# A shorter prologue and three short superblocks at the head of a banded-convolution, gate and two-projection kernel

## The chip, the cores and the metric

The kernel runs on one core of one Trainium2 chip. The metric is the device time of one execution in microseconds (us). Beside it each kernel has one profiled execution, whose trace gives the span from the first to the last instruction and the granted TensorE clock. PE is TensorE (PEld its weight loads), DVE VectorE, ACT ScalarE, POOL GpSimd, and SP the engine that here only issues DMAs. "Record" means one row of the trace.

## The reference

x is (8, 4224, 192) in float32. First a causal convolution of 7 taps with one kernel per head (8 heads of 24 channels, softmax over the taps), then a gated projection:

```python
# _attn_ref: w = softmax(weight, axis=-1); K = 7, H = 8
x_unf = x_pad[:, idx, :].reshape(B, S, K, H, group)
out = np.einsum('hk,bskhg->bshg', w, x_unf)
# _moe_ref on that output, K = 5
for k in range(K):
    gate_pre += conv_w[k][None, None, :] * xp[:, k:k + S, :]
gate = 1.0 / (1.0 + np.exp(-gate_pre))
val = x @ w_val
return (gate * val @ w_out).astype(np.float32)
```

x and the 7-tap weight are float32; conv_w, w_val and w_out are float64, and the kernel gets their bits as pairs of 32-bit words.

## The kernel before, in words

**Layout.** The eight sequences are laid end to end as two rows of 16926 tokens that run side by side. The 192 channels don't fit 128 partitions evenly: tile x1 holds 128 channels of both rows one behind the other, tile x2 the other 64 channels, row 0 on its lower 64 partitions and row 1 on its upper.

**Superblocks and steps.** The tokens are cut into superblocks g (list NJS; the number is windows of 122 tokens per fifth). A superblock of 5 has 1506 tokens in three steps of 502, of 3 has 896 in two steps of 448, of 2 has 606 in steps of 304 and 302. Before there are 13 superblocks and 35 steps.

**The convolution** (conv_unit) is a product with a band matrix: a window of 128 tokens by 120 columns (24 channels by 5 windows) is the stationary operand, the head's band (128x122) the moving one. Each such product is two records in the trace. Up to four windows form a unit in one bank of PSUM; ACT copies the unit to tile e, and when a head is complete, scatter sends it by DMA from e to x1 and x2: heads 0 to 4 in one transfer to x1, heads 5 to 7 in two or four smaller ones. A superblock of 5 has 40 such products (10 units), of 3 has 24 (6 units), of 2 has 16 (4 units). Heads go in the order QUADS: 6, 7, 5, 0, then 1, 2, 3, 4. The windows come from HBM by load_x into a ring of XBUFS buffers; load i waits until the products that read its buffer's former content are done.

**The main loop** runs over steps n. For step n PE makes the products v = x·w_val (three single-precision-rounded products for high and low parts, and a float32 part in columns), for step n-1 the products o with w_out; ACT opens and closes gates (gate_open scales by tap 0, gate_close is the sigmoid), DVE adds the other four taps (gate_taps) and multiplies (gated), POOL makes the low parts (split1, split2). Then come due[n] units of the convolution of the superblock LAG = 2 further on. gate_open(n+2, 0) stands in the middle of step n on ACT and waits for the scattered x1 of the superblock of step n+2. The order on each engine is that of the code, written out by hand.

**The prologue.** Band and weights are prepared: band is exp(taps - max), with -1e30 outside of the band, multiplied by 1/sum (rs). decode turns the float64 bits into a float32 value and a residual on DVE; put adds them into the weight tile; cast makes the rounded high part (ACT) and the low part (DVE). The convolution of superblocks 0 and 1 is interleaved with the decoding; then the loop begins.

```python
NJS = [2, 3] + [5] * 10 + [2]
PER_LOAD = {2: 2, 3: 1, 5: 1}
XBUFS, EBUFS = 6, 3
LAG = 2
BY_POOL = 3
```

Of the kernel before, what the change touches and what calls it, by code (L numbers as in the profile page):

```python
# [19 lines left out]
WIN = 122  # L20
# [8 lines left out]

NJS = [2, 3] + [5] * 10 + [2]


def half(n):
# [15 lines left out]
def room(n):  # L51
    return min(reach(n), NS * fifth(n)) - HALO
# [7 lines left out]
assert 0 < LEFT <= min(502, room(NJS[-1])) and LEFT % 2 == 0  # L60
NG = len(NJS)
PARTS = [BLOCKS[n] for n in NJS[:-1]] + [TAIL]
TOKS = [sum(p) for p in PARTS]
STEPS = []
# [16 lines left out]
PERM += [h * HC + i for i in range(HC) for h in (6, 7)]  # L81
PERM += [5 * HC + i for i in range(8, HC)]
QUADS = ((6, 7, 5, 0), (1, 2, 3, 4))
PER_LOAD = {2: 2, 3: 1, 5: 1}
XBUFS, EBUFS = 6, 3
LAG = 2
BY_POOL = 3


@with_exitstack  # L90
def kernel(
# [39 lines left out]
    def load_x(upto):  # L131
        while loaded[0] < min(upto, len(loads)):
            i = loaded[0]
            loaded[0] += 1
            g, hs, o = loads[i]
            f = len(hs) * NJS[g] * M
            t = xtiles[i] = xin.tile([WK, NMAX * M], F32, tag="x", name=f"x_{i}")
            nc.sync.dma_start(t[:, :f], xw[o : o + WK * f].rearrange("(p f) -> p f", f=f))

    w0 = cp.tile([128, NH, KW], F32, name="w0")
    nc.sync.dma_start(w0, hw)
    band = cp.tile([WK, NH, WIN], F32, name="band")
    for q in range(2):
        nc.sync.dma_start(band[:, 4 * q : 4 * q + 4, :], bw[:, 4 * q : 4 * q + 4, :])
# [15 lines left out]
    def load_raw(name):  # L162
        nc.sync.dma_start(raw[name][1], raw[name][2])

    load_raw("cw")
    load_raw("wv")
    load_x(4)
    load_raw("wo")
    load_x(XBUFS)

    one = cp.tile([128, 1], F32, name="one")
    nc.vector.memset(one, 1.0)
    warm = cp.tile([128, 1], F32, name="warm")
# [7 lines left out]
    nc.vector.tensor_reduce(out=mx, in_=w0, op=ALU.max, axis=mybir.AxisListType.X)  # L181
    w1 = cp.tile([128, NH, KW], F32, name="w1")
    nc.vector.tensor_tensor(out=w1, in0=w0, in1=wide(mx, KW), op=ALU.subtract)
    w2 = cp.tile([128, NH, KW], F32, name="w2")
    nc.scalar.activation(w2, w1, AF.Exp)
    halves = [slice(4 * q, 4 * q + 4) for q in range(2)]
    for q in halves:
        nc.vector.tensor_tensor(out=band[:, q], in0=band[:, q], in1=wide(mx, WIN, q), op=ALU.subtract)
        nc.scalar.activation(band[:, q], band[:, q], AF.Exp)
# [6 lines left out]
    for q in halves:  # L196
        nc.vector.tensor_tensor(out=band[:, q], in0=band[:, q], in1=wide(rs, WIN, q), op=ALU.mult)  # L197
    warm2 = cp.tile([128, 1], F32, name="warm2")
    nc.scalar.activation(warm2, rs[:, 0:1], AF.Sigmoid)

    tmp = [scratch(2 * D, 0 if i < 3 else 1) for i in range(4)]

    def decode(name, n):

        lo, hi = raw[name][0][:, :, 0], raw[name][0][:, :, 1]
        ex, ta, tb, res = (t[:, :n] for t in tmp)
        res = res.bitcast(F32)
        v = nc.vector
        SHR, SHL = ALU.logical_shift_right, ALU.logical_shift_left
        AND, OR, XOR = ALU.bitwise_and, ALU.bitwise_or, ALU.bitwise_xor  # L210

        v.tensor_scalar(out=ex, in0=hi, scalar1=20, scalar2=0x7FF, op0=SHR, op1=AND)
# [4 lines left out]
        v.scalar_tensor_tensor(out=ta, in0=ta, scalar=0x40000000, in1=tb, op0=XOR, op1=AND)
        v.tensor_tensor(out=ta, in0=ta, in1=ex, op=OR)
        v.scalar_tensor_tensor(out=ta, in0=hi, scalar=-0x80000000, in1=ta, op0=AND, op1=OR)

        v.tensor_scalar(out=tb, in0=ta, scalar1=-0x800000, scalar2=None, op0=AND)
        v.scalar_tensor_tensor(
            out=res, in0=lo.bitcast(U32), scalar=2.0**-52, in1=tb.bitcast(F32), op0=ALU.mult, op1=ALU.mult
        )
        return ta.bitcast(F32), res

    def put(dst, pr, p0, p1, c0, c1):
        nc.vector.tensor_tensor(out=dst, in0=pr[0][p0:p1, c0:c1], in1=pr[1][p0:p1, c0:c1], op=ALU.add)
# [42 lines left out]
    def conv_unit(u):  # L271
# [381 lines left out]
```

## Time and profile before

| | |
|---|---|
| median of 3 runs | 405.81 us (405.56 to 406.46) |
| profiled execution | 406.11 us, span 404.3 us, mean granted clock 0.974 |
| busy | PE 373.3, PEld 315.7, DVE 347.1, ACT 320.3, POOL 249.7 us |
| DMA | 82.49 MB, mean 204 GB/s over the span |
| largest DVE group | L359, the taps on pa: 172.1 us in 140 instructions |
| convolution on PE | L285: 912 records |

Busy time is a union: overlapping records count once. In the page's slices each digit is the busy share of a fortieth of the span in tenths, PEclk the granted clock in tenths. The stage table gives busy time with the number of records, then the granted clock, the mean busy share of the 16 DMA engines and what they moved. In rows of groups the numbers behind the bar are busy us and mean ns of one, then the idle time before them and what ended it.

### The profile page before, as it was taken

The numbers are of one execution on the slowest core, as the hardware profiler recorded it, in microseconds if no ns is written. First come the engines' busy times: TensorE is split into PE (matmuls) and PEld (weight loads), VectorE is DVE, ScalarE is ACT, GpSimd is POOL, SyncE is SP. The second block draws the span as 40 slices with busy tenths as digits, with TensorE's granted clock in tenths as the row PEclk, the third lists the DMA queues.
The fourth block names the chain that finished last, engine by engine and source line by source line (L and its number), as shares of the span: only waits on it lengthen the run. The fifth ranks groups of instructions, "written<-read, shape, count | busy, mean of one in ns | idle before, by whom it ended". The sixth has DMA issues, their size and how long they took to land.

```text
span 404.3 us, 8347 instructions
## 1 busy us (share of the span) xinstructions
PE 373.3 (92%) x3082; PEld 315.7 (78%) x3082; DVE 347.1 (86%) x435; ACT 320.3 (79%) x508; POOL 249.7 (62%) x170
## 2 busy tenths in 40 slices
PE   1685967999999999999999999999999999899896
PEld 1675966888888888888888888888888888676674
DVE  4888865689899899899999989989989989999971
ACT  4465937888888888888888988888888888788754
POOL 0834933666566666666666666666666656676772
PEclk9959996999999999999999999999999999999999
DMA  7697884886997897798698698698698696232233
GB/s 240 186 239 216 180 248 135 214 248 187 215 271 222 186 274 245 158 266 255 167 251 256 186 233 254 182 225 265 186 204 260 192 212 213 99 124 100 79 150 136
DMA packets 37884, 82.49 MB, mean 204 GB/s; under 512 B 5548, under 2 KB 16564, under 8 KB 37844
## 3 DMA queue, kind: packets, MB, share of 16 engines
q1 hardware_dynamic: 36756, 80.22, 70.0%
q0 software_dynamic: 1088, 1.74, 2.1%
q8 instruction: 24, 0.39, 0.5%
q14 instruction: 16, 0.13, 0.1%
HBM read 29.34 MB, written 26.00 MB: 137 GB/s over the span
## 4 chain that ended last, share of the span: by engine, by line
PE 85%; DMA 6%; DVE 4%; ACT 1%; issue 1%; SPq 1%; ACTq 0%; DVEq 0%
PE pc L285 22%; PE o L425 12%; PE v L425 11%; PE v L453 8%; PE o L453 7%; PE v L438 7%; PE o L438 6%; PE v L415 6%; PE o L415 6%; DMA x<-e 4%; DMA x<-xw 1%; DMA band<-bw 1%; DVE g L468 1%; DVE pa L359 1%; DVE pb L359 1%
## 5 line engine op out<-in xcount | busy, mean ns | idle before, releaser
L359 DVE SCALAR_TENSOR_TENSOR pa<-x,cwt,pa 128x1004 f32<-128x1004 f32 (+4 forms) x140 | 172.1, 1229 | 10.5 <-ACT pa L352 5.9
L285 PE MATMUL pc<-band,x 128*120 128x122 f32 x912 | 109.0, 279 | 20.8 <-DVE band L197 8.3
L285 PEld LDWEIGHTS pc<-band,x 128*120 128x120 f32 x912 | 107.1, 193 | 24.3 <-DVE band L197 8.3
L381 POOL TENSOR_TENSOR xl<-x,xh 128x1004 fp32r<-128x1004 f32 (+4 forms) x35 | 73.3, 2095 | 79.5 <-ACT xh L380 67.7
L359 DVE SCALAR_TENSOR_TENSOR pb<-x,cwt,pb 128x502 f32<-128x502 f32 (+4 forms) x140 | 101.3, 724 | 3.7
L468 DVE TENSOR_TENSOR g<-v,g 128x502 f32<-128x502 f32 (+4 forms) x105 | 65.6, 657 | 28.3 <-PE v L438 18.3
L381 POOL TENSOR_TENSOR pl<-g,ph 128x1004 fp32r<-128x1004 f32 (+4 forms) x35 | 79.0, 2256 | 7.8 <-ACT ph L380 6.7
L389 POOL TENSOR_TENSOR pl<-g,ph 128x502 fp32r<-128x502 f32 (+4 forms) x35 | 42.8, 1222 | 50.5 <-ACT ph L388 50.5
L372 ACT ACTIVATE g<-pa 128x1004 f32<-128x1004 f32 (+4 forms) x35 | 34.3, 980 | 46.2 <-DVE pa L359 20.6
L294 ACT COPY e<-pc 120x488 f32<-120x488 f32 x114 | 59.0, 587 | 6.7 <-PE pc L285 6.5
L484 ACT COPY ot<-o 128x502 f32<-128x502 f32 (+4 forms) x105 | 55.3, 561 | 1.6 <-PE o L425 0.9
L352 ACT ACTIVATE pa<-x,cwt 128x1004 f32<-128x1004 f32 (+4 forms) x35 | 37.5, 1072 | 14.8 <-DMA x<-e 9.6
L389 POOL TENSOR_TENSOR xl<-x,xh 128x502 fp32r<-128x502 f32 (+4 forms) x35 | 41.2, 1178 | 0.0
L453 PEld LDWEIGHTS v<-x,wvf 128*64 128x64 f32 x560 | 28.8, 136 | 12.0 <-issue 11.7
L453 PE MATMUL v<-x,wvf 128*64 128x125 f32 (+5 forms) x560 | 36.8, 272 | 0.0
L380 ACT CAST ph<-g 128x1004 fp32r<-128x1004 f32 (+4 forms) x35 | 34.9, 998 | 1.0 <-DVE g L468 1.0
L453 PE MATMUL o<-g,wof 128*64 128x125 f32 (+5 forms) x560 | 35.2, 266 | 0.0
L380 ACT CAST xh<-x 128x1004 fp32r<-128x1004 f32 (+4 forms) x35 | 34.4, 984 | 0.0
L453 PEld LDWEIGHTS o<-g,wof 128*64 128x64 f32 x560 | 30.6, 136 | 0.2 <-issue 0.2
L425 PE MATMUL o<-ph,woh 128*128 128x502 f32 (+4 forms) x70 | 30.4, 434 | 0.0
L425 PE MATMUL v<-xh,wvh 128*128 128x502 f32 (+4 forms) x70 | 27.4, 391 | 0.0
L425 PE MATMUL v<-xh,wvl 128*128 128x502 f32 (+4 forms) x70 | 27.3, 391 | 0.0
(74 smaller groups left out, 549.0 us busy)
## 6 DMA issues: line engine op xcount, KB each, us to landing
x<-xw SPq DMA_DIRECT2D x80, 300.0 KB
out<-ot SPq DMA_DIRECT2D x30, 753.0 KB
x<-e SPq DMA_DIRECT2D x50, 285.9 KB
x<-e SPq DMA_DIRECT2D x36, 141.6 KB
x<-xw SPq DMA_DIRECT2D x8, 240.0 KB
x<-e SPq DMA_DIRECT2D x18, 94.4 KB
x<-xw SPq DMA_DIRECT2D x8, 180.0 KB
out<-ot SPq DMA_DIRECT2D x2, 672.0 KB
```

Of the source, the lines that this page charges most:

```text
L285: nc.tensor.matmul(pc[:M, k * WIN : (k + 1) * WIN], lhsT=xtiles[i][:, c : c + M], rhs=band[:, 4 * q + hi, :], start=True, stop=True,)
L294: nc.scalar.copy(e[:, a : a + w], pc[:M, :w])
L359: nc.vector.scalar_tensor_tensor(out=acc, in0=views(n, k)[i], scalar=cwt[:, i, k : k + 1], in1=acc, op0=ALU.mult, op1=ALU.add,)
L380: nc.scalar.copy(h, x)
L381: nc.gpsimd.tensor_tensor(out=l, in0=x, in1=h.bitcast(F32), op=ALU.subtract)
L389: nc.gpsimd.tensor_tensor(out=l, in0=x, in1=h.bitcast(F32), op=ALU.subtract)
L415: nc.tensor.matmul(acc, lhsT=a[:, r], rhs=b, start=(i == 0), stop=False)
L425: nc.tensor.matmul(acc, lhsT=a[:, r], rhs=b[:, q], start=(fresh and i == 0), stop=(not fresh and i == 2))
L438: nc.tensor.matmul(acc, lhsT=a[p, r], rhs=b[p], start=(fresh and i == 0), stop=(not fresh and i == 2))
L453: nc.tensor.matmul(acc[p, c], lhsT=w.f[:, W12 : W12 + 64], rhs=x[:, q, c], start=False, stop=(i == 3),)
L468: nc.vector.tensor_tensor(out=v, in0=banks.pop(("v", n, q)), in1=v, op=ALU.mult)
L484: nc.scalar.copy(ots[n][:, q * m : (q + 1) * m], banks.pop(("o", n, q)))
```

## The change

The superblocks become 2, 3, 3, 3, eight of 5, 3, 3 (the last with 688 tokens): 14 superblocks, 36 steps. The number of convolution products (456) stays. Loads of superblocks of 3 carry two heads each (720 columns instead of 360); the ring has 8 buffers. The prologue: w0 and the second band half are fetched on ACT's queue; the subtraction of the maximum becomes the bias of eight exponentials, one per head; decode has seven operations instead of nine, and put three sums per weight instead of five, since the weight tile keeps its columns in the order of the data; 13 products with a zero tile stand first on PE; the table load for the sigmoid moved behind superblock 0's copies on ACT; heads 3 and 4 of superblock 0 are scattered on ACT's queue; the loads behind superblock 0 have an order of their own.

```diff
-NJS = [2, 3] + [5] * 10 + [2]
+NJS = [2, 3, 3, 3] + [5] * 8 + [3, 3]
-TAIL = (LEFT,)
+TAIL = (LEFT // 2, LEFT - LEFT // 2)
-PER_LOAD = {2: 2, 3: 1, 5: 1}
-XBUFS, EBUFS = 6, 3
+PER_LOAD = {2: 2, 3: 2, 5: 1}
+XBUFS, EBUFS = 8, 3
+WARM = 13
...
-    nc.sync.dma_start(w0, hw)
-    for q in range(2):
-        nc.sync.dma_start(band[:, 4 * q : 4 * q + 4, :], bw[:, 4 * q : 4 * q + 4, :])
-        if q == 0:
-            load_x(1)
+    nc.scalar.dma_start(w0, hw)
+    nc.sync.dma_start(band[:, halves[0]], bw[:, halves[0]])
+    nc.scalar.dma_start(band[:, halves[1]], bw[:, halves[1]])
+    load_x(2)
...
+    nc.vector.memset(zero, 0.0)
+    for i in range(WARM):
+        nc.tensor.matmul(pw[:M, :WIN], lhsT=zero[:, :M], rhs=zero[:, M:], start=True, stop=True)
...
+    nc.vector.tensor_scalar(out=nmx, in0=mx, scalar1=-1.0, scalar2=None, op0=ALU.mult)
-    for q in halves:
-        nc.vector.tensor_tensor(out=band[:, q], in0=band[:, q], in1=wide(mx, WIN, q), op=ALU.subtract)
-        nc.scalar.activation(band[:, q], band[:, q], AF.Exp)
+    for h in range(NH):
+        nc.scalar.activation(band[:, h], band[:, h], AF.Exp, bias=nmx[:, h : h + 1])
...
+        v.tensor_scalar(out=ta, in0=hi, scalar1=0x7FFFFFFF, scalar2=None, op0=AND)
+        v.tensor_scalar(out=tf, in0=tf, scalar1=LOW, scalar2=HIGH, op0=ALU.max, op1=ALU.min)
+        v.tensor_scalar(out=tb, in0=hi, scalar1=-0x80000000, scalar2=0x40000000, op0=AND, op1=XOR)
+        v.tensor_scalar(out=ta, in0=ta, scalar1=3, scalar2=0x7FFFFFFF, op0=SHL, op1=AND)
+        v.tensor_tensor(out=ta, in0=ta, in1=tb, op=XOR)
...
-            if last and g < BY_POOL:
+            if last and 0 < g < BY_POOL:
                 load_x(i + 1 + XBUFS)
+            if g == 0 and last:
+                load_x((5, 6, 8, 12)[i])
...
+        elif g == 0 and h in (3, 4):
+            dma = nc.scalar.dma_start
...
     conv(first_unit[1])
+    nc.scalar.activation(warm2, rs[:, 0:1], AF.Sigmoid)
     w_val.cast()
     conv(2)
     w_out.decode()
-    conv(1)
     gate_open(0, 0)
```

In the rows below, which give an engine's order, the name left of the arrow is written and those right of it are read: x_i is load i, x1_g the scattered tile of superblock g, e_g_q its convolved half q, pc a bank of the convolution, v_n_q and o_n_q the products of step n.

SP's queue from the first load of superblock 1 (x_4) to the first load of superblock 2 (x_12), before:

```order
L138 DMA x_4_109<-xw 128x360
L138 DMA x_5_111<-xw 128x360
L138 DMA x_6_183<-xw 128x360
L318 DMA x1_0_170<-e_0_0_172 24x5x244
L138 DMA x_7_196<-xw 128x360
L318 DMA x1_0_170<-e_0_1_198 24x5x244 x2
L138 DMA x_8_207<-xw 128x360
L318 DMA x1_0_170<-e_0_1_198 24x5x244 x2
L138 DMA x_9_217<-xw 128x360
L138 DMA x_10_232<-xw 128x360
L138 DMA x_11_242<-xw 128x360
L138 DMA x_12_268<-xw 128x600
```

and from x_4 after:

```order
L145 DMA x_4_109<-xw 128x720
L332 DMA x1_0_183<-e_0_0_185 24x5x244
L145 DMA x_5_207<-xw 128x720
L332 DMA x1_0_183<-e_0_1_209 24x5x244 x2
L145 DMA x_6_218<-xw 128x720
L145 DMA x_7_220<-xw 128x720
L145 DMA x_8_230<-xw 128x720
L145 DMA x_9_232<-xw 128x720
L145 DMA x_10_234<-xw 128x720
L145 DMA x_11_236<-xw 128x720
L145 DMA x_12_260<-xw 128x720
L332 DMA x1_1_241<-e_1_0_243 24x5x366
```

Two of superblock 0's scatters left this queue, and the loads of superblock 2 (8 to 11) and the first of superblock 3 (12) now stand ahead of superblock 1's first scatter here.

ACT's order in the prologue, before:

```order
L189 ACTIVATE band_92<-band_92 128x488 x2
L199 ACT_TABLE_LOAD
L199 ACTIVATE warm2_135<-rs_131 128x1
L294 COPY e_0_0_172<-pc_0_173 120x488
L294 COPY e_0_0_172<-pc_1_185 120x488
L294 COPY e_0_1_198<-pc_2_199 120x488
L294 COPY e_0_1_198<-pc_3_209 120x488
L255 CAST wvh_139<-wvf_138 128x384
```

and after:

```order
L203 ACTIVATE band_91<-band_91,nmx_135 128x122 x8
L301 COPY e_0_0_185<-pc_0_186 120x488
L301 COPY e_0_0_185<-pc_1_196 120x488
L301 COPY e_0_1_209<-pc_2_210 120x488
L301 COPY e_0_1_209<-pc_3_222 120x488
L332 DMA x1_0_183<-e_0_1_209 24x5x244 x2
L532 ACT_TABLE_LOAD
L532 ACTIVATE warm2_155<-rs_151 128x1
L262 CAST wvh_158<-wvf_157 128x448
```

The table load went behind the four copies, and two DMA issues came in ahead of the cast of w_val.

PE's order from the end of step 0's products to the start of step 1, before:

```order
L438 MATMUL v_0_1_352<-xl2_0_290,wvh_139 128x304
L285 MATMUL pc_10_394<-band_92,x_12_268 120x122 x4
L285 MATMUL pc_11_400<-band_92,x_12_268 120x122
L285 MATMUL pc_11_400<-band_92,x_13_271 120x122 x3
L285 MATMUL pc_12_410<-band_92,x_13_271 120x122 x2
L285 MATMUL pc_12_410<-band_92,x_14_303 120x122 x2
L285 MATMUL pc_13_420<-band_92,x_14_303 120x122 x3
L285 MATMUL pc_13_420<-band_92,x_15_312 120x122
L285 MATMUL pc_14_432<-band_92,x_15_312 120x122 x4
L415 MATMUL v_1_2_445<-xh2_1_344,wvh_139 128x302
```

and after:

```order
L452 MATMUL v_0_1_360<-xl2_0_289,wvh_158 128x304
L292 MATMUL pc_10_402<-band_91,x_8_230 120x122 x4
L292 MATMUL pc_11_410<-band_91,x_8_230 120x122 x2
L292 MATMUL pc_11_410<-band_91,x_9_232 120x122 x2
L292 MATMUL pc_12_420<-band_91,x_9_232 120x122 x4
L429 MATMUL v_1_2_437<-xh2_1_352,wvh_158 128x302
```

Step 0 now carries 12 products of superblock 2 (24 records) from two loads, instead of 20 (40 records) from four.

More of the change, by code (lines that the diff above doesn't have):

```diff
@@ L58 @@
 LEFT = TOTAL - sum(sum(BLOCKS[n]) for n in NJS[:-1])
-TAIL = (LEFT,)
-assert 0 < LEFT <= min(502, room(NJS[-1])) and LEFT % 2 == 0
+TAIL = (LEFT // 2, LEFT - LEFT // 2)
+assert 0 < LEFT <= room(NJS[-1]) and LEFT % 4 == 0 and max(TAIL) <= 502
 NG = len(NJS)
+LOW = 2.0**-15
+HIGH = 1.875 * 2.0**16
 PARTS = [BLOCKS[n] for n in NJS[:-1]] + [TAIL]
@@ L83 @@
 QUADS = ((6, 7, 5, 0), (1, 2, 3, 4))
-PER_LOAD = {2: 2, 3: 1, 5: 1}
-XBUFS, EBUFS = 6, 3
+PER_LOAD = {2: 2, 3: 2, 5: 1}
+XBUFS, EBUFS = 8, 3
+XW = max(PER_LOAD[n] * n * M for n in NJS)
 LAG = 2
 BY_POOL = 3
+WARM = 13
 @with_exitstack
@@ L136, in load_x @@
             f = len(hs) * NJS[g] * M
-            t = xtiles[i] = xin.tile([WK, NMAX * M], F32, tag="x", name=f"x_{i}")
+            t = xtiles[i] = xin.tile([WK, XW], F32, tag="x", name=f"x_{i}")
             nc.sync.dma_start(t[:, :f], xw[o : o + WK * f].rearrange("(p f) -> p f", f=f))
     w0 = cp.tile([128, NH, KW], F32, name="w0")
-    nc.sync.dma_start(w0, hw)
     band = cp.tile([WK, NH, WIN], F32, name="band")
-    for q in range(2):
-        nc.sync.dma_start(band[:, 4 * q : 4 * q + 4, :], bw[:, 4 * q : 4 * q + 4, :])
-        if q == 0:
-            load_x(1)
+    halves = [slice(4 * q, 4 * q + 4) for q in range(2)]
+    nc.scalar.dma_start(w0, hw)
+    nc.sync.dma_start(band[:, halves[0]], bw[:, halves[0]])
+    nc.scalar.dma_start(band[:, halves[1]], bw[:, halves[1]])
+    load_x(2)
     scr = [op.tile([128, 3 * MB], F32, tag="ot", name=f"scr_{i}") for i in range(3)]
@@ L168 @@
     load_raw("wo")
-    load_x(XBUFS)
+    load_x(5)
     one = cp.tile([128, 1], F32, name="one")
     nc.vector.memset(one, 1.0)
+    zero = cp.tile([WK, M + WIN], F32, name="zero")
+    nc.vector.memset(zero, 0.0)
     warm = cp.tile([128, 1], F32, name="warm")
     nc.scalar.activation(warm, one, AF.Exp)
+    for i in range(WARM):
+        if i == 0:
+            pw = ps.tile([128, 512], F32, tag="p", name="pw")
+        nc.tensor.matmul(pw[:M, :WIN], lhsT=zero[:, :M], rhs=zero[:, M:], start=True, stop=True)
     def wide(t, k, q=slice(0, NH)):
@@ L183 @@
     nc.vector.tensor_tensor(out=w1, in0=w0, in1=wide(mx, KW), op=ALU.subtract)
+    nmx = cp.tile([128, NH], F32, name="nmx")
+    nc.vector.tensor_scalar(out=nmx, in0=mx, scalar1=-1.0, scalar2=None, op0=ALU.mult)
     w2 = cp.tile([128, NH, KW], F32, name="w2")
     nc.scalar.activation(w2, w1, AF.Exp)
-    halves = [slice(4 * q, 4 * q + 4) for q in range(2)]
-    for q in halves:
-        nc.vector.tensor_tensor(out=band[:, q], in0=band[:, q], in1=wide(mx, WIN, q), op=ALU.subtract)
-        nc.scalar.activation(band[:, q], band[:, q], AF.Exp)
+    for h in range(NH):
+        nc.scalar.activation(band[:, h], band[:, h], AF.Exp, bias=nmx[:, h : h + 1])
     sm = cp.tile([128, NH], F32, name="sm")
@@ L238, in __init__ @@
             self.name = name
-            self.f = cp.tile([128, NW + 64], F32, name=f"{name}f")
+            self.f = cp.tile([128, NW], F32, name=f"{name}f")
             self.h = cp.tile([128, NW], F32R, name=f"{name}h")
@@ L310, in scatter @@
         x1, x2 = x1s[g], x2s[g]
-        dma = nc.gpsimd.dma_start if g < BY_POOL and h >= 5 else nc.sync.dma_start
+        if g < BY_POOL and h >= 5:
+            dma = nc.gpsimd.dma_start
+        elif g == 0 and h in (3, 4):
+            dma = nc.scalar.dma_start
+        else:
+            dma = nc.sync.dma_start
         def rows(c0, c1):
```

31 lines of the change are left out of this document (11 added, 20 removed).

## The prediction

> **What bounds the kernel now.** I read the page's forty slices first, then busy time by stage, then the chain of waits, then the timeline where the chain leaves PE.
>
> ```profile
> PE   1685967999999999999999999999999999899896
> PEclk9959996999999999999999999999999999999999
> DMA  7697884886997897798698698698698696232233
> ```
>
> PE is full from the eighth slice to the end; only the first seven slices (71 us), and a little at the end, have holes. By stage:
>
> ```profile
> core 0: us, PE busy (x) PEld busy (x) DVE busy (x) ACT busy (x) POOL busy (x), PEclk, DMA share, GB/s
> 0.00:8.27 8.27, 0.00 (x0) 0.00 (x0) 3.03 (x10) 3.69 (x6) 0.55 (x6) 1.00 0.70 210
> 26.49:49.68 23.19, 19.07 (x175) 17.71 (x175) 19.49 (x29) 16.66 (x31) 13.87 (x16) 0.88 0.81 204
> 49.68:80.42 30.74, 24.76 (x208) 22.71 (x207) 18.95 (x23) 19.09 (x33) 13.86 (x9) 0.89 0.72 201
> 112.18:334.50 222.32, 222.32 (x1864) 187.86 (x1863) 204.71 (x232) 193.78 (x302) 145.04 (x85) 1.00 0.81 225
> 334.50:404.30 69.80, 62.27 (x497) 48.17 (x495) 57.18 (x69) 51.02 (x80) 44.48 (x27) 1.00 0.36 128
> 0.00:36.36 36.36, 21.49 (x151) 20.15 (x151) 27.77 (x69) 16.62 (x30) 14.86 (x26) 0.86 0.84 232
> ```
>
> The middle is PE from end to end. So the change can pay only before 80.42 and after 334.5, and there must not cost the middle anything. The chain of waits, in order of time:
>
> ```profile
> 2.13 4.05 DMA band<-bw
> 29.52 6.83 DMA x<-e
> 54.04 7.50 DMA x<-e
> 63.59 5.23 PE pc L285 x24
> 76.22 4.20 PE pc L285 x40
> 98.34 3.36 PE pc L285 x32
> 320.75 3.36 PE pc L285 x32
> 331.85 2.52 PE pc L285 x24
> ```
>
> Two scatters hold the ramp: superblock 1's last rows land at 36.35, superblock 2's at 61.54. The timeline shows who waits:
>
> ```profile
> 2.13 0.43 SPq L146 DMA_DIRECT2D band<-bw  x1
> 8.27 7.09 PE L285 MATMUL pc<-band,x 128*120 128x122 f32 x50 [8.27 <-DVE band L197]
> 8.71 0.17 DVE L212 TENSOR_SCALAR scr<-scr 128x10 int32<-128x10 int32 x1
> 10.51 0.35 DVE L212 TENSOR_SCALAR scr<-scr 128x384 int32<-128x384 int32 x1
> 14.74 0.99 DVE L228 TENSOR_TENSOR wvf<-scr,scr 128x128 f32<-128x128 f32 x5
> 22.89 3.53 DVE L359 SCALAR_TENSOR_TENSOR pa<-x,cwt,pa 128x608 f32<-128x608 f32 x4 [0.84 <-DMA x<-xw]
> 29.52 0.79 SPq L318 DMA_DIRECT2D x<-e  x1
> 34.31 2.24 DVE L359 SCALAR_TENSOR_TENSOR pb<-x,cwt,pb 128x302 f32<-128x302 f32 x4
> 36.58 1.01 ACT L352 ACTIVATE pa<-x,cwt 128x896 f32<-128x896 f32 x1 [2.62 <-DMA x<-e]
> 39.07 0.62 PE L415 MATMUL v<-xh,wvh 128*128 128x302 f32 x1 [2.61 <-ACT e L294]
> 49.70 0.45 PE L415 MATMUL v<-xh,wvh 128*128 128x448 f32 x1
> 61.64 1.10 ACT L352 ACTIVATE pa<-x,cwt 128x1004 f32<-128x1004 f32 x1 [6.96 <-DMA x<-e]
> ```
>
> ACT stands in its queue for x1 (2.62 and 6.96 us); behind it wait the copies that free PE's banks (39.07) and DVE. Step 2 starts at 49.70, step 4 at 76.22+4.20=80.42, step 28 at 334.37.
>
> **Prices.** A convolution record at full clock is 3.36/32=0.105 us (half clock: 5.23/24=0.218). Seven superblocks of three steps take 320.75-98.34=222.41, so 31.77 each; less 80 records (8.40), a 502-step's products cost 7.79. By columns a 448-step costs 6.95, 344 5.34, 302 4.69.
>
> ```profile
> L359 DVE SCALAR_TENSOR_TENSOR pa<-x,cwt,pa 128x896 f32<-128x896 f32 x8 | 9.2, 1155 | 1.3 <-ACT pa L352 1.1
> L359 DVE SCALAR_TENSOR_TENSOR pb<-x,cwt,pb 128x448 f32<-128x448 f32 x8 | 5.5, 687 | 0.2
> L468 DVE TENSOR_TENSOR g<-v,g 128x448 f32<-128x448 f32 x6 | 3.6, 622 | 7.1 <-PE v L453 5.5 <-PE v L438 1.6
> L189 ACT ACTIVATE band<-band 128x488 f32<-128x488 f32 x2 | 1.2, 609 | 3.0 <-DVE band L188 3.0
> L185 ACT ACTIVATE w<-w 128x56 f32<-128x56 f32 x1 | 0.2, 249 | 0.8 <-DVE w L183 0.8
> L217 DVE SCALAR_TENSOR_TENSOR scr<-scr 128x384 int32<-128x384 int32 x2 | 1.1, 558 | 0.1
> L199 ACT ACT_TABLE_LOAD x1 | 1.3, 1283 | 0.0
> x<-xw SPq DMA_DIRECT2D x80, 300.0 KB
> x<-e SPq DMA_DIRECT2D x50, 285.9 KB
> x<-e POOLq DMA_DIRECT2D x4, 57.2 KB, 2.3
> ```
>
> A 448-step costs DVE 4x1.155+4x0.687+3x0.622=9.24.
>
> **Prologue.** The first band half is now SP's first transfer and the second is ACT's second. Before they were SP's second and fourth, at 0.43 us an issue, so each goes out some 0.5 to 1 us sooner; with the row's 4.05 from issue to landing both are in by 4.0 to 5.2. Eight exponentials of 122 columns replace two subtractions on DVE and two exponentials. Between 0.249 (56 columns) and 0.609 (488) I take 0.31 each, so four cost 1.2; they start when the half has landed, since nmx is ready by about 3.2. The first product with rs (0.67 before, the same form) then ends near 5.9, and PE starts there, not at 8.27; the second half is ready by 7.1.
>
> The 13 zero matmuls stand ahead of the convolution in PE's queue. They are 26 records, at 0.218 5.7 us from about 1.2, and end by 6.9: at worst they hold PE back 1 us, at best they save the half-clock price on superblock 0's 32 records (3.6 us). I put either at nothing, because those records then wait for loads 2 and 3 and for ACT's copies, and nothing later hangs on them; if that cover went, the +1 would stand.
>
> The decode of wv took DVE 14.74+0.99-10.51=5.22. Two 0.56 operations with their gaps (1.18) go, and two of five sums (0.4): 3.6. For cwt eight small operations of 0.17 and a gap take 1.5, so wv is decoded at about 7.1+1.5+3.6=12.2. DVE then waits for the cast. On ACT two scatter issues (0.79 each on SP, taken for ACT too) and the table load (1.283) now stand between the last copy of superblock 0, near 10.3, and the cast; behind them also wait the copies of superblock 1. The cast ends near 14.0, wvl at 14.6, wo at 18.2. The casts of the wider weights (448 columns for 384) cost 0.1 in all.
>
> So the taps of step 0 start at 18.2 instead of 22.89, 4.7 sooner, if superblock 0's rows have landed by 16: POOL issues its eight from about 7.6 to 12.5, and they took 2.3 (57.2 KB). By the same DVE sequence the taps of step 2 could start at 34.31+2.24-4.7=31.9. On POOL the scatter of head 5 of superblock 1 moved behind the two subtractions of step 0; it goes out near 22 instead of 17, still ahead of the last SP scatter.
>
> **When superblock 1 lands (L1).** Before, 232 GB/s over 36.36 us moved 8.44 MB. Ahead of the last scatter now go, by tile sizes, 1.3 MB of tables and weights, loads 0 to 3 (0.98), eleven of 128x720 (4.06), and both scatters (2.34): 8.7 MB. At full share the same row makes 232/0.84=276 GB/s; earlier and paired loads, with eight buffers for six, fill the holes (the chain's first two microseconds can't be filled), so I take a share of 0.95: L1=33.2. The loads are queued ahead of the scatters on SP, in one queue in order, so a scatter can't pass them; that is why their bytes count. Ends: 31.9, where DVE decides, and 36.3, no better than now. So DMA, not DVE, sets it, by 1.3 us; the prologue's 4.7 us are worth 3.
>
> **The ramp.** Before, step 2 started 13.3 after the landing, with 40 records in step 1; 24 now save 1.7: 11.6. Step 2 costs PE 3.5+2.35+2.5=8.35, step 3 6.95+2.5=9.5. DVE's 9.24 is almost the same, so I add 1.0 for small waits: step 4 starts at L1+30.5=63.7, against 80.42. This is the change's gain, 16.7: superblock 2 scatters 1.37 MB instead of 2.3, and its last copies are done near 45, so that its x1 is in by about 49, before ACT asks near 52; the 6.96 wait and the half clock behind it (2.7) go.
>
> **Given back.** 64 convolution records (6.7 us) that were done before step 4 are now behind it. Steps 4 to 7 carry 40 records each: 4x(6.95+4.2)=44.6. They need, per two steps, 8x300+8x285.9 KB and two outs of 672: 6.18 MB in 22.3 us, 277 GB/s where the middle's row makes 225/0.81=278 at full share. No reserve, and ACT asks for x1 half a step after its convolution: a wait of 0 (buffers hold) to 6.96 (as now); I take 2.5, nearer to nothing because eight loads are ahead instead of six. Steps 8 to 25 are 6x31.77=190.6, unchanged. The end, from step 26: 3.9 for the step before, six steps of 7.79, two of 6.95, two of 5.34, 96 records (10.1): 85.3. The present end has 59.6 by the same prices and takes 69.8, since DVE lags: 10 lost. The same again (8 to 13): 95.3.
>
> **The sum.** 63.7+44.6+2.5+190.6+95.3=396.7. The profiled run took 406.11 with a span of 404.3, so 398.5; the median is 0.3 lower than that run, which I leave in the rounding.
>
> **Rivals.** First, more: L1 at 31.9, no wait in steps 4 to 7, 8 lost at the end: 398.5-1.3-2.5-2=392.7. For it speaks DMA's idle share of 0.16 before 36.36; against it that every queue there is in order.
> Second, less: short superblocks mean smaller pieces. The stage from 26.49 made 204/0.81=252 GB/s at full share against 278 in the middle. At 252, L1 is 36.3 (+3.1) and the wait of steps 4 to 7 doubles (+2.5): 404.1. The Trainium skill, DMA: Bandwidth & Descriptors, section Rules for kernel authors, says small transfers should be joined into large ones, and that below 64 KB one pays mostly overhead; by that rule this rival is the likely one, and the 252 agrees with it in direction.
> Third, slower: ACT's wait for x1 returns. Superblocks of two steps give a scatter half a step before gate_open asks, which is where the 6.96 arose; at steps 6 and 8 that is two waits of 6.96+2.7=9.7 each: 396.7-2.5+19.3, with 1.8 beside the span 415.3. From 9.8 us of such waits in all, the kernel is slower. Against it: superblocks 1 to 3 hold 60% of a full one's bytes. The Trainium skill, TensorE: Matmul & The Clock Gate, Part 1, has the clock back after some 3.4 us of work, which would make the price 1.7 instead of 2.7; the 5.23 us at half clock in this trace say longer.
>
> **Chances.** Forecast 0.56 (its own range 395 to 401.5), more 0.20, less 0.14, slower 0.10. 0.2% is about what a measurement can tell from no change; 0.03 of the last two lies there. Faster 0.87, same 0.03, slower 0.10. The range 391.5 to 405 leaves out the tails of the first and the third.
>
> **What would show it.** PE's first convolution near 6, step 0's taps near 18, superblock 1's x1 wait over near 33, no wait over 2 us for superblock 2, step 4 near 64, PE full from there to step 26. Wrong if ACT waits for x1 in steps 4 to 7 by more than 5 us, if DVE starts its taps after 20, or if the end stage loses over 13.

## The result and the profile after

The changed kernel is slower. Its median is 415.45 us (415.35 to 415.64, 4 runs) against 405.69 us (405.39 to 406.46, 4 runs) for the kernel before: ratio 1.0238, 95% interval 1.022 to 1.0256. Ratios here and below are of means, and leave out three single executions further down, which lie more than 1.5% above the fastest run of their kernel. The forecast was 398.5 us. The profiled execution took 415.47 us with a span of 413.7 us (before 404.3) at a mean granted clock of 0.962 (before 0.974).

The page's slices of the changed kernel, each 10.3 us wide:

```profile
PE   8483999599399999999999999999999999999996
PEclk9686899989789999999999999999999999999999
DMA  7995646479379879869869869869869934334223
```

PE is busy in the first slice and in slices 6 and 7, where it had holes before. But holes remain in slices 2 to 4 (the waits for superblocks 0 and 1), and there are new ones at slices 8 and 11 (72 to 83 us and 103 to 114 us), in which DMA is busy only at four and three tenths. The same by stage, cut where PE starts superblock 0's convolution (6.86), where ACT gets superblock 1 (37.47), and at steps 2, 4, 8 and 26:

```profile
core 0: us, PE busy (x) PEld busy (x) DVE busy (x) ACT busy (x) POOL busy (x), PEclk, DMA share, GB/s
0.00:6.86 6.86, 5.65 (x28) 5.65 (x29) 2.24 (x10) 4.04 (x11) 0.55 (x6) 1.00 0.75 255
0.00:37.47 37.47, 24.02 (x164) 22.71 (x164) 24.43 (x59) 17.61 (x36) 14.77 (x26) 0.82 0.89 250
49.03:68.89 19.86, 19.13 (x173) 16.41 (x173) 18.05 (x23) 16.28 (x29) 14.65 (x11) 1.00 0.51 158
68.89:128.63 59.74, 48.56 (x410) 43.87 (x409) 38.09 (x46) 38.61 (x65) 26.64 (x17) 0.91 0.70 199
128.63:319.11 190.48, 190.48 (x1597) 161.06 (x1597) 174.01 (x198) 165.94 (x258) 123.39 (x72) 1.00 0.84 226
319.11:413.70 94.59, 89.35 (x747) 71.90 (x746) 81.94 (x102) 74.42 (x121) 62.41 (x39) 1.00 0.43 147
```

Steps 8 to 25 are full on PE and last 190.48 us; the end stage lasts 94.59. The loss is above them: steps 4 to 7 take 59.74 us and hold 48.56 of PE's work, with the granted clock at 0.91. The DMA share there is 0.70, so bandwidth as an average is not what runs out.

Rows of the changed kernel's chain of waits, in order of time:

```profile
6.86 3.58 PE pc L292 x32
12.62 7.59 DMA x<-e
30.32 7.15 DMA x<-xw
66.37 2.52 PE pc L292 x24
74.35 5.12 DMA x<-e
81.70 4.49 PE pc L292 x24
101.66 9.12 DMA x<-e
113.07 4.37 PE pc L292 x24
```

The four DMAs in these rows each end just before ACT opens a superblock; three of them are the last scatters of superblocks 0, 3 and 4. The row at 30.32 is named a load, which this opening doesn't read: SP issued superblock 1's last two scatters from 27.35 to 28.96 us, so at least 8.5 us passed before ACT opened at 37.48. The last scatter of superblock 0 (114 KB) goes out at 12.62 and takes 7.59 us, beside seven 360 KB loads that SP issues from 12.59. Superblock 4's last scatter takes 9.12 us. The timeline shows who stood behind them; the bracket is the idle time before the row and what ended it:

```profile
20.36 0.77 ACT L366 ACTIVATE pa<-x,cwt 128x608 f32<-128x608 f32 x1 [3.11 <-DMA x<-xw]
21.16 3.53 DVE L373 SCALAR_TENSOR_TENSOR pa<-x,cwt,pa 128x608 f32<-128x608 f32 x4 [1.34 <-ACT pa L366]
37.48 1.01 ACT L366 ACTIVATE pa<-x,cwt 128x896 f32<-128x896 f32 x1 [5.25 <-DMA x<-xw]
79.72 1.01 ACT L366 ACTIVATE pa<-x,cwt 128x896 f32<-128x896 f32 x1 [5.68 <-DMA x<-e]
81.70 4.49 PE L292 MATMUL pc<-band,x 128*120 128x122 f32 x24 [4.15 <-ACT ot L498]
111.00 1.10 ACT L366 ACTIVATE pa<-x,cwt 128x1004 f32<-128x1004 f32 x1 [8.46 <-DMA x<-e]
113.07 4.37 PE L292 MATMUL pc<-band,x 128*120 128x122 f32 x24 [7.03 <-ACT ot L498]
```

ACT stands in its queue for x1 of superblocks 3 and 4 (5.68 and 8.46 us, 14.1 together). Its copies of o, which free PE's banks, stand behind that wait, so PE stands 4.15 and 7.03 us. After each hole 24 convolution records take 4.49 and 4.37 us instead of 2.52. That accounts for the stage: the 44.6 us of work in the forecast, 11.2 of standing, and 1.97 + 1.85 of slow clock give 59.6, against 59.7 measured.

One stretch of SP's queue in the changed kernel, while superblock 4 is scattered, shows how the transfers are mixed:

```profile
95.50 1.66 SPq L145 DMA_DIRECT2D x<-xw  x1
97.24 0.82 SPq L332 DMA_DIRECT2D x<-e  x1
98.16 0.47 SPq L145 DMA_DIRECT2D x<-xw  x1
98.72 0.78 SPq L332 DMA_DIRECT2D x<-e  x1
99.60 0.49 SPq L145 DMA_DIRECT2D x<-xw  x1
100.18 0.79 SPq L332 DMA_DIRECT2D x<-e  x1
101.07 0.49 SPq L145 DMA_DIRECT2D x<-xw  x1
101.66 0.96 SPq L332 DMA_DIRECT2D x<-e  x1
```

Ahead of each scatter stands a load for superblock 5; of the 1.66 us at 95.50, 1.1 are a wait for PE to release that load's buffer. ACT's last copy for superblock 4 was done at 98.0; the scatter that carries it goes out 3.7 us later and lands at 110.8, 12.8 us after the copy.

### The profile page after: what moved, and what is told of

Its sections match the earlier page's. It is cut to its first block, busy times and chain, and to the rows that moved or that the text cites. A ratio compares the mean times of both kernels' runs of the same rounds, so it can differ in the third digit from the quotient of the medians.

```text
span 413.7 us, 8583 instructions
## 1 busy us (share of the span) xinstructions
PE 381.6 (92%) x3170; PEld 325.0 (79%) x3170; DVE 345.5 (84%) x436; ACT 323.3 (78%) x525; POOL 251.9 (61%) x174
## 4 chain that ended last, share of the span: by engine, by line
PE 79%; DMA 9%; DVE 6%; ACT 3%; issue 2%; ACTq 0%; SPq 0%; DVEq 0%
PE pc L292 20%; PE o L439 11%; PE v L439 10%; PE v L467 8%; DMA x<-e 7%; PE v L452 6%; PE o L467 6%; PE o L429 5%; PE o L452 5%; PE v L429 5%; DMA x<-xw 3%; DVE pa L373 2%; DVE pb L373 2%; PE pw L188 1%; DVE g L482 1%
## 5 line engine op out<-in xcount | busy, mean ns | idle before, releaser
L292 PE MATMUL pc<-band,x 128*120 128x122 f32 x912 | 109.6, 279 | 20.1 <-ACT ot L498 11.8
L395 POOL TENSOR_TENSOR xl<-x,xh 128x1004 fp32r<-128x1004 f32 (+4 forms) x36 | 74.7, 2074 | 79.2 <-ACT xh L394 70.8
L467 PEld LDWEIGHTS v<-x,wvf 128*64 128x64 f32 x576 | 29.5, 138 | 11.8 <-issue 11.8
L467 PE MATMUL v<-x,wvf 128*64 128x126 f32 (+4 forms) x576 | 37.6, 273 | 0.0
L467 PE MATMUL o<-g,wof 128*64 128x126 f32 (+4 forms) x576 | 35.9, 266 | 0.0
L439 PE MATMUL v<-xl,wvh 128*128 128x502 f32 (+4 forms) x72 | 27.3, 379 | 0.0
```

Source lines behind the costliest of these rows:

```text
L292: nc.tensor.matmul(pc[:M, k * WIN : (k + 1) * WIN], lhsT=xtiles[i][:, c : c + M], rhs=band[:, 4 * q + hi, :], start=True, stop=True,)
L395: nc.gpsimd.tensor_tensor(out=l, in0=x, in1=h.bitcast(F32), op=ALU.subtract)
L439: nc.tensor.matmul(acc, lhsT=a[:, r], rhs=b[:, q], start=(fresh and i == 0), stop=(not fresh and i == 2))
L467: nc.tensor.matmul(acc[p, c], lhsT=w.f[:, W12 : W12 + 64], rhs=x[:, q, c], start=False, stop=(i == 3),)
```

## The experiments

All times are medians, with the ratio to the kernel before on the same chip and its 95% interval. Edits are to the changed kernel unless said otherwise.

**Two halves of the change.** The new prologue, loads and ring with the old superblocks:

```diff
-NJS = [2, 3, 3, 3] + [5] * 8 + [3, 3]
-TAIL = (LEFT // 2, LEFT - LEFT // 2)
+NJS = [2, 3] + [5] * 10 + [2]
+TAIL = (LEFT,)
```

> The new prologue, eight buffers, paired loads for superblocks of 3, but the superblocks of before (2, 3, ten of 5, 2). Theory A (the loss lies in the superblocks of two steps that follow one another): superblock 1's x1 lands at 36 to 37.5 as in the changed kernel, one wait for superblock 2 of 6 to 8 us as before, none for 3 and 4: 403 to 407 us, no slower than before. Theory B (the prologue costs: zero matmuls, table load and DMA issues on ACT, many loads ahead): over 410 us.

Measured: 406.35 us, 1.0003 (0.9977 to 1.0029). The whole prologue, which was to bring step 0's taps 4.7 us forward, gives nothing. ACT opens superblock 1 at 36.69 (before 36.58), and then waits 7.64 us for superblock 2 (before 6.96).

The old prologue, single loads and ring of six with the new superblocks (the opposite edit, on the kernel before):

> The prologue, buffers and single loads of before, but the new superblocks (2, 3, 3, 3, eight of 5, 3, 3). Theory A: the two waits of ACT for x1 of superblocks 3 and 4, in steps 4 and 6, of 5 to 9 us each: 413 to 418 us. Theory B: at most 406.

Measured: 416.79 us, 1.0269 (1.0233 to 1.0305). The whole loss comes with the new cut. ACT's two long waits in this kernel's timeline, for superblocks 3 and 4:

```profile
81.15 1.01 ACT L352 ACTIVATE pa<-x,cwt 128x896 f32<-128x896 f32 x1 [9.72 <-DMA x<-e]
112.12 1.10 ACT L352 ACTIVATE pa<-x,cwt 128x1004 f32<-128x1004 f32 x1 [8.25 <-DMA x<-e]
```

ACT opens superblock 1 at 33.55 here, near the 33.2 that the forecast had for the changed kernel, with the prologue that the change replaces. So the forecast's L1 (the landing of superblock 1) was reachable, but not with the new order of loads, and an early L1 alone doesn't help: the wait for superblock 3 is then 9.72 instead of 5.68.

**Fewer loads ahead of superblock 1.** The load targets while superblocks 0 and 1 are scattered are lowered:

```diff
-                load_x((5, 6, 8, 12)[i])
+                load_x((5, 6, 7, 8)[i])
...
-                load_x(i + 1 + XBUFS)
+                load_x(i + 6 if g == 1 else i + 1 + XBUFS)
```

> The changed kernel with loads 8 to 12 taken out from between superblock 0's and superblock 1's scatters on SP: they are issued one by one behind superblock 1's heads. If the bytes queued ahead of a scatter set when it lands: superblock 0's x1 is complete near 17 instead of 20, the taps of step 0 start at 18 to 19 instead of 21.2, superblock 1's x1 lands at 31 to 34 instead of 37.5, and the time falls by 2 to 5 us to 410 to 413; the waits in steps 4 and 6 stay. If a scatter's own latency sets it: 415 and no move of the two landings.

Measured: 413.57 us, 1.02 (1.0145 to 1.0255). Superblock 1 lands 2.6 us sooner (34.9 for 37.5), just outside the expected 31 to 34; the waits for superblocks 3 and 4 stay (6.26 and 8.32). The interval overlaps that of the changed kernel, so a gain in time isn't shown.

**More time for the scatters.** All convolution of superblocks 3 and 4 put into the first of the two steps that carry it:

```diff
+            if g in (3, 4) and at[n + 1] > a:
+                share = 1.0
             total += round(share * (first_unit[g + 1] - first_unit[g]))
```

> The changed kernel, but all units of superblocks 3 and 4 are convolved in the first of the two steps of the superblock two before (steps 2 and 4), so that a scatter has a step and a half before ACT asks, and nothing in those two superblocks is left for steps 3 and 5. Theory A (half a step of slack is the cause): both waits fall below 2 us, step 8 starts 10 to 14 us sooner, 401 to 406 us. Theory C (the DMAs as a whole are too slow for superblocks of two steps): the waits come back elsewhere, 411 us or more.

Measured: 411.05 us, 1.0149 (1.0093 to 1.0206). The waits fall to 1.60 and 4.76 us, not to nothing: superblock 4's last scatter still goes out at 97.37, because SP is busy with its scatters and loads from 82.4 to 98.2.

The other way round, ACT asks later: gate_open(n+2, 0) moved behind the convolution's copies for n = 0, 2, 4, 6.

```diff
-        gate_open(n + 2, 0)
+        if n not in LATE:
+            gate_open(n + 2, 0)
...
         conv(todo)
+        if n in LATE:
+            gate_open(n + 2, 0)
```

> The changed kernel, but in steps 0, 2, 4 and 6 ACT opens the gate of the step after next behind that step's convolution copies instead of in the middle, so that nothing else of the step stands behind the wait for x1. If the loss is that ACT's queue blocks (the copies that free PE's banks and the casts for the o products stand behind the wait): PE is no longer held in steps 4 and 6, each wait costs 3 to 5 us less, 406 to 410 us. If the loss is the late x1 itself (DVE has nothing to tap until it lands): DVE waits instead, 413 to 415 us.

Measured: 410.26 us, 1.01 (1.0061 to 1.0139). ACT's waits for superblocks 2 to 4 are gone from the timeline, and 5 us come back, a little less than expected. Part of the wait has moved: from 60 to 125 us DVE stands 9.1 us ahead of its taps for ACT's opening.

**Loads behind the scatters.** For superblocks 3 and 4 the loads are issued behind the last head's scatter (in one go) instead of one ahead of each head's:

```diff
-            if last and g >= BY_POOL:
+            if last and g >= BY_POOL and g not in (3, 4):
                 load_x(i + 1 + XBUFS)
             scatter(g, h, e[:, hi * n * WIN : (hi + 1) * n * WIN])
...
+            if g in (3, 4) and h == 4:
+                load_x(i + 1 + XBUFS)
```

> The changed kernel, but for superblocks 3 and 4 no load of a later superblock is issued until all scatters of the superblock are. If loads interleaved with the scatters in SP's queue and on the DMA engines make the scatters late: x1 of superblock 3 lands 2 to 4 us sooner and that of 4 4 to 8 us sooner, 405 to 410 us, with possibly a wait of PE for loads of superblock 5 of 1 to 3 us. If not: 414 to 417 us, since only the loads come later.

Measured: 403.62 us, 0.9953 (0.993 to 0.9976), below the expected range. The order of at most twelve loads is worth 11.8 us against the changed kernel. From this kernel's timeline, SP's issues for superblock 4 and ACT's openings of superblocks 3 and 4:

```profile
90.72 3.42 SPq L334 DMA_DIRECT2D x<-e  x4
94.23 5.67 SPq L145 DMA_DIRECT2D x<-xw  x8
75.74 1.01 ACT L368 ACTIVATE pa<-x,cwt 128x896 f32<-128x896 f32 x1 [2.98 <-DMA x<-xw]
99.70 1.10 ACT L368 ACTIVATE pa<-x,cwt 128x1004 f32<-128x1004 f32 x1 [2.40 <-DMA x<-e]
```

The four last scatters go out back to back, the eight loads follow, and the waits fall from 5.68 and 8.46 to 2.98 and 2.40.

**Turn in the queue, or bytes on the engines?** Loads ahead of a scatter can delay it in two ways: SP issues in order, about 0.5 us a load and 0.8 a scatter, and the loads' bytes then share the 16 DMA engines with the scatter. Three kernels tell these apart. First the small scatters (heads 5 to 7) of superblocks 3 and 4 go by POOL, which shortens SP's list but moves the same bytes (BY_POOL = 5 instead of 3; with it these superblocks' loads stand behind their heads' scatters):

> The changed kernel, but the eight small scatters (heads 5 to 7) of superblocks 3 and 4 go through POOL's queue, as those of superblocks 0 to 2 do, instead of SP's. If SP's time to issue (0.8 us a scatter, one behind the other, while the DMA engines are only 35% busy from 56 to 68) makes the last scatters late: the wait of 5.7 for superblock 3 falls below 2, that of 8.5 for 4 to 4 to 6, 406 to 411 us. If the transfers themselves are too slow: 414 us or more.

Measured: 412.67 us, 1.0165 (1.0125 to 1.0204), between the two ranges. The wait for superblock 3 falls to 2.38, that for superblock 4 stays at 8.70; its last scatter takes 10.15 us from issue to landing.

Then the same twelve loads, at their places in the code, issued by POOL, or by ACT:

```diff
...
             if last and g >= BY_POOL:
-                load_x(i + 1 + XBUFS)
+                load_x(i + 1 + XBUFS, nc.gpsimd if g in (3, 4) else nc.sync)
...
```

> The changed kernel, with the loads that are issued during the convolution of superblocks 3 and 4 (twelve) on POOL's queue instead of SP's, at the same places of the code. Theory one, the turn in SP's queue: the scatters no longer stand behind the loads' issues, so the last scatter of superblock 4 goes out within 2 us of its last copy and lands within 8 of it; ACT's waits for x1 of superblocks 3 and 4 fall from 5.7 and 8.5 to 3 and 3.5 or less, as when the loads stood behind; time 402.5 to 407. Theory two, the shared DMA engines: the loads' bytes delay the scatters whoever issues them; the waits stay at 5 to 9 and the time at 412 to 417.

Measured: 411.77 us, 1.0145 (1.0115 to 1.0176), with waits of 5.41 and 6.50. The second half of superblock 4's scatters here, from the timeline and (last but one row) the chain of waits:

```profile
94.68 4.51 SPq L332 DMA_DIRECT2D x<-e  x4
95.03 2.18 POOL L145 DMA_DIRECT2D x<-xw  x4
96.14 0.57 ACT L301 COPY e<-pc 120x488 f32<-120x488 f32 x1 [0.27 <-PE pc L292]
98.42 9.24 DMA x<-e
107.76 1.10 ACT L366 ACTIVATE pa<-x,cwt 128x1004 f32<-128x1004 f32 x1 [6.50 <-DMA x<-e]
```

SP now issues its four scatters without a load between them, and the last goes out 1.7 us after the last copy (96.14 + 0.57), as theory one wants. But it takes 9.24 us to land, as it did at 9.12 with the loads in SP's queue; in the kernel with the loads behind the scatters it takes 6.15. So theory one is right about the issue and wrong about the time: freeing the queue is worth 3.7 us of the 11.8, and the other 8 came back where the loads start later. The Trainium skill, DMA: Bandwidth & Descriptors, section Issuing engines are not separate DMA queues, says that DMAs started by different engines run on the same 16 DMA engines and interleave, and that another issuer saves only the sequencer's time; the 9.24 beside 9.12 agrees.

How busy the engines are meanwhile doesn't explain the landing, though. While superblock 4's last scatter is in flight, in the changed kernel, with the loads on POOL, and with the loads behind (columns of the stage table):

```profile
101.66:110.78 9.12, 4.38 (x34) 3.73 (x32) 3.82 (x6) 0.88 (x1) 1.66 (x2) 0.93 0.62 179
98.42:107.66 9.24, 6.34 (x67) 5.49 (x66) 4.55 (x8) 1.65 (x3) 3.21 (x2) 1.00 0.73 224
93.36:99.51 6.15, 5.77 (x57) 4.49 (x55) 4.06 (x7) 2.75 (x4) 3.23 (x2) 1.00 0.90 236
```

The scatter is fastest where the DMA share is highest, 0.90, and there the loads were issued behind it; in the changed kernel the share from 108 to 110 us is 0.18, with the scatter still to land. So in these runs loads issued ahead of a scatter lengthen it, from SP's queue or POOL's, and loads issued behind it do so less, if at all; what happens on the engines between is not shown.

With the same loads on ACT's queue:

> The same twelve loads on ACT's queue, at the same places. Theory one: the x1 waits fall as with POOL's queue, but ACT pays about 0.5 us for each issue, 6 us in all, part of it in time in which it waited for x1 before; 403 to 409. Theory two: the waits stay and the issues come on top: 414 to 420.

Measured: 412.23 us, 1.0152 (1.0123 to 1.0182); waits of 3.65 and 5.91. This falls between the two ranges. SP's four last scatters take 8.61 us to issue here though no load stands in its queue. What SP waits for from 88 to 101 us (total, times, longest):

```profile
SPq L332 <- DMA out<-ot: 4.2, 1, 4.2
SPq L332 <- DMA x<-e: 1.8, 4, 0.8
```

The last scatter stands 4.2 us until the 672 KB of results (out) that SP issued at 90.61 have landed; it goes out at 99.38, three us behind ACT's last load, and takes 6.46 us. So a turn in SP's queue can also cost the landing of an earlier transfer. The chains of the runs with fewer loads ahead and with the new superblocks alone have the same: superblock 4's last scatter goes out as an out transfer of 6.5 us lands.

Last, each load just behind its own head's scatter, on SP:

> The changed kernel, with each load of that stage issued just behind the scatter of the same head instead of just ahead of it, all on SP. Theory one, the turn in the queue: a scatter still stands behind the loads of the heads before it, only its own is out of the way, 0.5 to 1 us at the last one: waits about 5 and 7.5, time 411 to 415. Theory three, that only the load directly ahead of a scatter holds it: waits 3 or less, time 402 to 406.

Measured: 415.54 us, 1.0226 (1.0187 to 1.0264), with waits of 5.03 and 8.40: no change against the changed kernel. Swapping neighbours does nothing; the last scatter still goes out with loads ahead of it and takes 9.60 us. What helped was to put all loads behind the last scatter.

**Zero products.** The 13 products with the zero tile, and its memset, left out:

> The changed kernel without the 13 zero matmuls. PE's first convolution starts near 6.2 instead of 6.86, its 32 records run at about 0.22 us each instead of 0.11 if the zero matmuls were what brought the clock up (superblock 0 done near 13 instead of 10.4), and the time is the same within 1 us (414.5 to 416.5) if the waits for x1 behind it set the end; by 1 to 3 us longer if superblock 0's rows then land later.

Measured: 417.99 us, 1.0285 (1.0241 to 1.0329). That is 2.5 us above the changed kernel's 415.45, but the two intervals overlap a little, so a gain in time from the zero products is likely and not shown. The first convolution starts sooner without them, but runs slower; in that kernel's timeline:

```profile
6.39 7.70 PE L286 MATMUL pc<-band,x 128*120 128x122 f32 x44 [6.39 <-DVE band L205]
```

and in the changed kernel's:

```profile
6.65 5.04 PE L292 MATMUL pc<-band,x 128*120 128x122 f32 x44
```

The 44 records take 7.70 us against 5.04, so superblock 0's last copy ends 2.4 us later (13.4 for 11.0) and ACT opens step 0 at 22.73 instead of 20.36.

**Better versions.** Fewer loads ahead of superblock 1 together with loads behind the scatters, for superblocks 2, 3 and 4:

```diff
-            if last and g >= BY_POOL:
+            if last and g >= BY_POOL and g not in (2, 3, 4):
...
-            if last and 0 < g < BY_POOL:
-                load_x(i + 1 + XBUFS)
+            if last and 0 < g < BY_POOL and g not in (2, 3, 4):
+                load_x(i + 6 if g == 1 else i + 1 + XBUFS)
+            if g in (2, 3, 4) and h == 4:
+                load_x(i + 1 + XBUFS)
...
-                load_x((5, 6, 8, 12)[i])
+                load_x((5, 6, 7, 8)[i])
```

> The changed kernel with both orders of loads: fewer ahead of superblock 1's scatters, and for superblocks 2, 3 and 4 no load issued until all the superblock's scatters are. If both losses are loads ahead of scatters in one queue, the gains add up: 403.6 of the run with loads behind the scatters, less 1.5 to 2.5: 400 to 402.5 us. If the second takes the first's place: 403 to 406.

Measured: 401.78 us (399.49 to 403.83), 0.9889 (0.9836 to 0.9942): 1.1% faster than the kernel before and 3.3% faster than the changed one, with the change's own superblocks and prologue. Its profiled execution took 399.49 us, the fastest of four, with a span of 397.7. Steps 4 to 7 of this kernel, and the stage up to ACT's start of superblock 1, with the columns of the stage table:

```profile
65.02:112.54 47.52, 45.96 (x411) 40.83 (x410) 38.10 (x46) 38.33 (x65) 26.81 (x17) 1.00 0.79 248
0.00:34.56 34.56, 23.63 (x164) 21.98 (x164) 24.53 (x59) 17.57 (x36) 14.76 (x26) 0.85 0.81 231
```

and its last scatter of superblock 4 in the chain of waits, with ACT's opening:

```profile
89.62 6.25 DMA x<-e
96.06 1.10 ACT L368 ACTIVATE pa<-x,cwt 128x1004 f32<-128x1004 f32 x1 [2.65 <-DMA x<-e]
```

Steps 4 to 7 take 47.52 us instead of 59.74, at full clock and 248 GB/s instead of 199. The later loads cost little: in step 6 PE waits 1.2 us for one.

The same with the late opening of steps 2, 4, 6 and 8 on top:

> The same with ACT's late opening in steps 0, 2, 4 and 6. If what is left of the waits still blocks ACT's queue, 1 to 3 us less than without: 397 to 401 us, faster than before by 1 to 2%. If the late opening only moves the wait to DVE: 400 to 403 us.

Measured: 408.73 us, 1.0081 (1.0045 to 1.0117): 7 us slower than without it, and outside both ranges. Two remedies for one wait don't add; once x1 is there in time, the late opening only delays DVE. DVE's taps on pa between 45 and 120 us, first of this kernel:

```profile
L376 DVE SCALAR_TENSOR_TENSOR pa<-x,cwt,pa 128x896 f32<-128x896 f32 (+1 forms) x27 | 32.0, 1184 | 10.6 <-ACT pa L369 6.1 <-DMA x<-e 3.8
```

and without the late opening:

```profile
L375 DVE SCALAR_TENSOR_TENSOR pa<-x,cwt,pa 128x896 f32<-128x896 f32 (+1 forms) x28 | 33.2, 1187 | 0.7
```

DVE stands 10.6 us ahead of its taps, 6.1 of it for ACT's opening, and PE then stands four times for g (3.47, 1.70, 1.70 and 2.26 us).

Last, the old superblocks with the new prologue, to see whether the new cut is needed at all. With fewer loads ahead and the late opening for n = 0 and 2:

> The superblocks of before (2, 3, ten of 5, 2) with the new prologue, the loads ahead cut as in the run with fewer loads ahead, and ACT's late opening in steps 0 and 2. If loads ahead and ACT's block are what took the prologue's gain: superblock 1's x1 lands at 32 to 34 instead of 36.7, the wait for superblock 2 is outside PE's way, 398 to 403 us, faster than before. If the DMA total sets the ramp whatever the order: 404 to 407 us.

Measured: 403.81 us (399.66 to 405.97), 0.9926 (0.9897 to 0.9954). ACT opens superblock 1 at 36.50, not at 32 to 34; what is left of the wait for superblock 2 is 0.66 us, since ACT asks later. And with superblock 2's loads behind its scatters as well:

> The superblocks of before with the new prologue, fewer loads ahead, superblock 2's scatters ahead of all loads of superblock 3, and ACT's late opening in steps 0 and 2. If loads between the scatters also made the wait of 7 us of the kernel before: superblock 2's x1 lands near 55 to 58 instead of 61.5, 398 to 401 us. If not: 403 to 406 us, as with the tuned prologue alone.

Measured: 402.72 us (400.32 to 406.98), 0.991 (0.9884 to 0.9937), between the two ranges and not clear of the run before it; ACT asks for superblock 2 so late that its landing can't be read. The interval overlaps that of the best version (0.9836 to 0.9942), so these runs do not show that short superblocks gain anything over the old ones, once the loads are ordered for each.

## Why the prediction was wrong, point by point

The span is 413.7 where the sum had 396.7: 17.0 us. By the sum's own terms: L1 +4.3, from L1 to step 4 +0.9, steps 4 to 7 +12.6, steps 8 to 25 -0.1, the end -0.7.

- **Prologue: near, but on the wrong chain.** PE's convolution started at 6.86, since the zero products ran to 6.85 and the first band half was ready at 6.22 (nmx came at 4.2 where 3.2 was taken): the forecast's 5.9 with its "at worst 1 us". The cast of w_val ended at 15.4 (forecast 14.0); the two scatter issues ahead of it on ACT took 2.36 us for the 1.58 assumed. Step 0's taps started at 21.16, not 18.2: DVE was still decoding until 19.8, and then stood 1.34 us more because superblock 0's rows landed at 20.2 and not "by 16". The price of those scatters was too low: I took the 2.3 us of the small ones from POOL, but the last one to land is a 114 KB scatter that took 7.59 us beside seven loads, and here the small ones took up to 7 us too. Taps later than 20 was one of the three marks named beforehand.
- **Zero products: wrong.** They were put at nothing because the first records would wait for loads and copies anyway. They ran at once, and with the zero products ahead superblock 0's copies end 2.4 us sooner; the medians differ by 2.5 us, which the intervals don't quite separate. The Trainium skill, TensorE: Matmul & The Clock Gate, Part 1, says that the clock is set by how busy PE has lately been, over a window of some 3.4 us, and not by a count of instructions; the 5.04 us for 44 records behind 5.64 us of products on zeros, against 7.70 without, agrees.
- **L1: wrong by 4.3.** It was 37.5, beyond the upper end of 36.3. The bytes and the share were misjudged together: by the stage row 250 GB/s over 37.47 us are 9.4 MB for the forecast's 8.7, at a share of 0.89 for 0.95. The eleven paired loads that the forecast counted are the ones issued ahead; SP issued two more from 29.06 us on, 0.68 MB by their tiles, which is about what the bytes are short (an estimate). With fewer loads ahead L1 was 34.9, and 33.55 with the old prologue and single loads, which fits the forecast's remark that loads ahead of the scatters count; but with the old superblocks fewer loads ahead moved ACT's opening only from 36.69 to 36.50.
- **From L1 to step 4: right.** 31.4 for 30.5, with a wait of 1.72 us for superblock 2, under the 2 named; step 4 starts 11.5 us sooner than before (68.9 for 80.42), as against the 16.7 forecast.
- **Steps 4 to 7: the step that failed.** The term was 44.6 plus a wait of 2.5. The work was right; the wait was mis-sized, at 11.2 plus 3.8 us of slow clock. The bounds "0 to 6.96" rested on one wait; there were two, and one is longer than any of before. The reason given for the lower half, eight loads ahead instead of six, is the reverse of what the runs show: loads ahead are what holds the scatters. "No reserve" at 277 GB/s was not the limit either: the stage ran at a share of 0.70, and in the best version, with the loads behind the scatters, it moved 248 GB/s and took 47.5 us, close to the forecast's 44.6 + 2.5 = 47.1.
- **Steps 8 to 25 and the end: right.** 190.5 for 190.6 and 94.6 for 95.3; the end lost 9.3 us against its priced work, for the 10 carried over.
- **The rivals.** The third, with two returning x1 waits in this place and 415.3 us, is what happened, and its argument (half a step of slack in a superblock of two steps) was the right one: longer slack by earlier units took the waits to 1.60 and 4.76. It gave the waits 19.3 us where 15.0 were lost; the other 4.3 are L1's, so that its 415.3 lies next to the measured 415.45 is in part luck. The argument set against it, that short superblocks scatter fewer bytes, does not hold for superblock 4, which is a full one but whose convolution has just two short steps, and neglects the loads issued ahead of the scatters.

With the loads put behind, the best version's profiled span of 397.7 is within 1.0 us of the forecast sum, from nearly the same terms: L1 34.6 (33.2), step 4 at 65.0 (63.7), steps 4 to 7 47.5 (47.1). That is its fastest run of four; its median of 401.78 is 3.3 us above the forecast. So the sum priced, within some 3 us, a kernel whose transfers are ordered by need, and the changed kernel's aren't.

What stays open: by what on the DMA engines a load issued ahead lengthens a scatter, and how much the out transfers, which SP also issues ahead of the last scatters, add to it. No kernel was run that leaves the loads in place and halves their bytes, or that moves the out transfers.

## What to carry to other kernels

When tiles are cut shorter, the time between the last producer and the first consumer of a transfer shrinks with them; list for each such transfer what else is in flight then, and issue prefetches that are needed later behind it, not ahead. Moving the prefetch to another engine's queue takes back only the issue time (3.7 of 11.8 us here). Two remedies for the same wait must be tried together before both are kept: the second may only delay the next engine.

## What the runs showed of the hardware beyond the expected

A 114 KB scatter took 7.59 us beside seven loads. Superblock 4's last scatter (286 KB) took 8.9 to 10.2 us with loads issued just ahead of it, and 6.2 to 6.3 in the two kernels with them behind and no late opening. And from 92 to 104 us the changed kernel kept the DMA engines at a share of 0.97 and moved 243 GB/s, where the middle makes 226 at 0.84:

```profile
92.00:104.00 12.00, 12.00 (x107) 10.86 (x106) 9.79 (x13) 8.90 (x16) 6.59 (x5) 1.00 0.97 243
```

That is 251 GB/s at full share against 269, while the best version moved 325 GB/s at the same share of 0.97 in its own 92 to 104 us, when its eight loads were under way. So what the engines move at full share differs from stretch to stretch (251 to 335 GB/s here); the cause was not measured.

The granted clock can't be read in the first microseconds: the stage row up to 6.86 gives 1.00, but the 26 zero records in it take

```profile
1.21 5.64 PE pw L188 x26
```

0.217 us each, the price at half clock (0.218), and the 32 behind them 3.58/32 = 0.112. There the durations of like records say more than the clock's column.
